# One eighth of w1 by five small loads, and selection tables set up by GpSimd, in a one-token attention and MLP kernel

## The chip, the cores and the metric

The kernel runs on one core of a Trainium2 chip. The metric is the device time of one execution in microseconds (us); the kernel before has a median of 401.98 us over 3 runs (401.95 to 402.12).

## The reference, cut to what matters

One token (`x`, 1024 wide, bf16) goes through an attention with a long cache and, side by side, through an MLP block; the three terms are added.

```python
xn = layernorm(x)
# A: 32 query heads on 4 key/value heads, 65536 cached keys of 128 each
q = xn @ wq                                   # 1024 x 4096
o = softmax(q k^T * 128**-0.5) v              # per head
A = o @ wo                                    # 4096 x 1024
# B: with S = 1
h = gelu(layernorm(xn) @ w1)                  # 1024 x 1024
hs = shift_and_pad(h) @ w2                    # quarters of h shifted by 1, -1, 2, -2 rows: all zero for S = 1
x1 = xn + hs
B = x1 + gelu(layernorm(x1) @ w3) @ w4        # 1024 x 3584, 3584 x 1024
out = x + A + B
```

Nothing is reused between tokens, so every weight and every cached key and value is read from HBM once: 169.87 MB.

## The kernel before, in words

SBUF holds three slots of 64 KB per partition (`SLOTS`, L15; L146). A list of items (L193 to L201) says what passes through them, in this order: `wq`, keys and values of the first half of group 0, `w3`, keys and values of its second half, `wa` (w1 and the first half of w4), then keys and values of the other six half groups, with `wb` (second half of w4, and w2) ahead of the last values, and `wo` last, in five pieces (L17). Each key or value item is 8 MB, 64 KB for each of 128 partitions.

**Loads.** All of them are issued by SyncE (SP) in `load` (L211 to L232, the DMA call itself at L89), in the order of the list, each as soon as the item three places before it has been computed. SP waits until the slot's readers are done (L229) and then issues; so two older loads are normally still queued when a new one is issued. Each `dma_start` adds 16 to a semaphore of its own slot and piece when it has landed. Two small loads of `x` are issued by ScalarE at the start: `x_bf` (L240) into 128 partitions and `xr` (L244) into two partitions, 1 KB each. The result leaves through a store from four partitions (L561).

**Order of engines.** `Flow` records every instruction with what it reads and writes and puts a wait on the engine when the last writer or reader was another engine or a DMA (L41 to L72). Each engine works through its own instructions in the order of the program.

**Items.** For keys, VectorE transposes the slot in blocks (L449), TensorE multiplies with the query (L455), VectorE takes the maximum (L462), ScalarE the exponential (L471), and VectorE transposes the weights (L473); for values, TensorE accumulates (L503). `group_end` (L513) joins the two halves of a group and uses the PSUM tile `pm` (L521 to L526). `compute_wq`, `compute_w3` and `compute_wa` multiply the one row of x, kept spread over partitions in `xpad`, with a weight whose row 8p + c lies in partition p, place c (`rows_product`, L310, matmul at L321): eight places c, and a matmul per place and chunk of 512 columns. In `compute_wa` (L405) this is w1 with 8 x 2 matmuls; then Gelu on ScalarE (L410), a cleared row on GpSimd (L411), a spreading matmul with `gsel` (L419), and the first half of w4 in a loop (`rows_loop`, L326, matmul at L337).

**Set-up.** GpSimd clears tiles and makes two identities (L243 to L260). VectorE makes masks (L265 to L274), then from the bf16 identity the selection tables `psel` (L278, four copies), `hstrip` (L283) and `gsel` (L285). `psel` is first read by the matmul at L368, `hstrip` at L394, `gsel` at L419.

**The end.** `compute_wo` (L541) takes the five pieces of wo as they land; after the last piece come four matmuls (L536), one VectorE copy (L560) and the store (L561).

Of the kernel before, what the change touches and what calls it, by code (L numbers as in the profile page):

```python
# [7 lines left out]
BF16 = mybir.dt.bfloat16  # L8
# [8 lines left out]
WO_PIECES = (10, 10, 8, 3, 1)  # L17
WO_UNROLL = 5
CGS = 2


class Flow:
# [51 lines left out]
    def op(self, eng, reads, writes, emit, times=1):  # L74

        self._wait(eng, reads, writes)
        sem = self.sem(eng)

        def signal(ins):
            ins.then_inc(sem, 1)  # L80

        emit(signal)
        self.counts[eng] += times
        self._note((eng, self.counts[eng]), reads, writes)
# [8 lines left out]
    def one(self, eng, reads, writes, call):  # L93
        self.op(eng, reads, writes, lambda signal: signal(call(self.engines[eng])))
# [3 lines left out]
def kernel(  # L98
# [14 lines left out]
    nc = tc.nc  # L113
    P = 128
    S = A_x.shape[1]
    D = A_x.shape[-1]
# [6 lines left out]
    DC = D // P  # L123
# [18 lines left out]
    def tile_sb(shape, dtype, name):  # L142
        return sb.tile(shape, dtype, name=name)
# [9 lines left out]
    ident_bf = tile_sb([P, P], BF16, "ident_bf")  # L153
# [3 lines left out]
    hstrip = tile_sb([P, 192], BF16, "hstrip")  # L157
    gsel = tile_sb([P, P], BF16, "gsel")
# [10 lines left out]
    xn2b = tile_sb([P, DC], BF16, "xn2b")  # L169
# [3 lines left out]
    gT = tile_sb([P, DC], BF16, "gT")  # L173
    o5 = tile_sb([P, 32], F32, "o5")
    oT = tile_sb([P, OC], BF16, "oT")
    rep = msk[0:1].rearrange("p a b -> p (a b)")

    sc = ps.tile([P, HF, 512], F32, name="sc")
    oacc = ps.tile([P, 512], F32, name="oacc")
    pm = ps.tile([P, 512], F32, name="pm")  # L180
# [4 lines left out]
    w3_v = B_w3.rearrange("(p c) f -> p (c f)", c=DC)  # L185
    w4_v = B_w4.rearrange("(m c) n -> m (c n)", c=FC)
    wo_v = A_wo.rearrange("(m c) n -> m (c n)", c=OC)
    w1_v = B_w1.rearrange("(p c) n -> p (c n)", c=DC)
    w2_v = B_w2.rearrange("(m c) n -> m (c n)", c=DC)
    assert sum(WO_PIECES) == OC  # L190
    wo_start = [sum(WO_PIECES[:i]) for i in range(len(WO_PIECES))]
# [13 lines left out]
    fl = Flow(nc, ctx)  # L205
    one, op = fl.one, fl.op
# [4 lines left out]
    def load(i):  # L211
        item, s = items[i], slot_of[i]
        t, kind = slots[s], items[i][0]
        if kind == "wq":
            loads = [(0, wq_v)]
        elif kind == "w3":
            loads = [(0, w3_v)]
        elif kind == "wa":
            loads = [(0, w1_v), (KEYS // 2, w4_v[:, 0:FH * NOUT])]
        elif kind == "wb":  # L220
            loads = [(0, w4_v[:, FH * NOUT:FC * NOUT]), (KEYS // 2, w2_v)]
        elif kind == "wo":
            loads = [(wo_start[q] * NOUT, wo_v[:, wo_start[q] * NOUT:(wo_start[q] + n) * NOUT])
                     for q, n in enumerate(WO_PIECES)]
        else:
            cache = A_k_cache if kind == "K" else A_v_cache
            _, g, r = item
            loads = [(0, cache[0, g, r * KEYS:(r + 1) * KEYS, :].rearrange("(p k) d -> p (k d)", p=P))]
        fl._wait("Q", [], [("slot", s), ("slot", s, 1)] + [("slot", s, q) for q in range(2, 5)] + [("kt", s, cg) for cg in range(4)])  # L229
        for n, (at, src) in enumerate(loads):  # L230
            key = ("slot", s) if n == 0 else ("slot", s, n)
            fl.dma("Q", f"slot{s}" if n == 0 else f"slot{s}_{n}", [], [key], t[:, at:at + src.shape[-1]], src)  # L232

    qrow = work[:, 0:1024].rearrange("p (b n) -> p b n", b=2)
    psel = work[:, 1024:1536].rearrange("p (b m) -> p b m", b=4)
    ones_f = og[:, 0:P]
    xr = work[:, 1536:2048]

    load(0)
    fl.dma("S", "x", [], ["x_bf"], x_bf[:], A_x[0, 0, :].rearrange("(p c) -> p c", c=DC))  # L240
    load(1)
    load(2)
    one("G", [], ["xr"], lambda e: e.memset(xr[0:33, :], 0.0))  # L243
    fl.dma("S", "x2", [], ["xr"], xr[0:33:32, :], A_x[0, 0, :].rearrange("(j n) -> j n", j=2))  # L244
# [17 lines left out]
    def v(reads, writes, call):  # L262
        one("V", reads, writes, call)
# [10 lines left out]
                                                   in_=sel8[:].unsqueeze(2).to_broadcast([P, 8, 4])))  # L274
    iv = ident_bf[:].rearrange("p (b i r) -> p b r i", b=2, r=2)
    for b in range(2):
        for par in range(2):
            v(["ident_bf"], [("psel", b, par)], lambda e: e.tensor_copy(  # L278
                out=psel[:, 2 * b + par, :].rearrange("p (a i) -> p a i", a=4),
                in_=iv[:, b, par, :].unsqueeze(1).to_broadcast([P, 4, 32])))  # L280
    psel_keys = [("psel", b, par) for b in range(2) for par in range(2)]
    lead = ident_bf[:].rearrange("p (j u) -> p j u", u=32)[:, :, 0]
    v(["ident_bf", "hstrip"], ["hstrip"], lambda e: e.tensor_copy(  # L283
        out=hstrip[:, 64:128].rearrange("p (j m) -> p j m", j=4), in_=lead.unsqueeze(2).to_broadcast([P, 4, 16])))
    v(["ident_bf"], ["gsel"], lambda e: e.tensor_copy(  # L285
        out=gsel[:].rearrange("p (j m) -> p j m", j=2), in_=lead[:, 0:2].unsqueeze(2).to_broadcast([P, 2, 64])))

    def layernorm(src, src_key, n):
# [22 lines left out]
    v([("rs", 0)], ["ln_s1"], lambda e: e.tensor_scalar(out=ln_s1, in0=rs1, scalar1=1.0, scalar2=None, op0=ALU.add))  # L311
    v([("neg", 0), ("rs", 0)], ["ln_s2"], lambda e: e.tensor_tensor(out=ln_s2, in0=neg1, in1=rs1, op=ALU.mult))

    def rows_product(s, keys, wt, width, n_chunks):
        def emit(signal):
            for c in range(DC):
                for j in range(4):
                    for bk in range(2):
                        ch = 4 * bk + j
                        if ch < n_chunks:  # L320
                            ins = nc.tensor.matmul(sc[32 * j:32 * j + 32, bk, 0:width], lhsT=xpad[:, c, :],  # L321
                                                   rhs=wt[:, c, ch * width:(ch + 1) * width],
                                                   start=(c == 0), stop=(c == DC - 1), tile_position=(0, 32 * j),
                                                   skip_group_check=True)
            signal(ins)
        op("T", keys + ["xpad"], ["sc"], emit)  # L326

    def rows_loop(lhsT, wt, n, reads, unroll):

        lv = lhsT.rearrange("p (c u) -> p c u", u=unroll)  # L330
        wv = wt.rearrange("p (c u h n) -> p c u h n", u=unroll, h=2, n=NH)

        def emit(signal):
            with nc.tensor.Fori(0, n // unroll) as c:
                for u in range(unroll):
                    for h in range(2):
                        ins = nc.tensor.matmul(psR[0:1, h, :], lhsT=lv[:, bass.ds(c, 1), u],  # L337
                                               rhs=wv[:, bass.ds(c, 1), u, h, :],
                                               start=False, stop=False, skip_group_check=True)
                signal(ins)  # L340
        op("T", reads, ["psR"], emit, times=n // unroll)
# [62 lines left out]

    def compute_wa(s):  # L405
        slot = slots[s]
        wt = slot[:, 0:DC * D].rearrange("p (c n) -> p c n", n=D)
        rows_product(s, [("slot", s)], wt, 512, 2)
        h1row, grow = work[0:64, 0:512], work[0:64, 512:1024]
        one("S", ["sc"], ["h1row", "work"], lambda e: e.activation(out=h1row, in_=sc[0:64, 0, :], func=ACTF.Gelu_apprx_tanh))  # L410
        one("G", [], ["grow", "work"], lambda e: e.memset(grow, 0.0))  # L411
        cq = D // 4
        for grp, shift in enumerate((1, -1, 2, -2)):
            for t in range(S):
                if 0 <= t - shift < S:
                    r0, c0 = 32 * (grp // 2), cq * (grp % 2)
                    v(["h1row", "grow"], ["grow"], lambda e: e.tensor_copy(
                        out=grow[r0:r0 + 1, c0:c0 + cq], in_=h1row[r0:r0 + 1, c0:c0 + cq]))
        one("T", ["grow", "gsel"], ["pm"], lambda e: e.matmul(pm[:], lhsT=gsel[0:64, :], rhs=grow, start=True, stop=True))  # L419
        gm = work[:, 1024:2048].bitcast(F32).rearrange("p (a c) -> p a c", c=DC)  # L420
        v(["pm", "mask64"], ["gm"], lambda e: e.tensor_tensor(
            out=gm, in0=pm[:].rearrange("p (a c) -> p a c", c=DC),
            in1=mask64[:].unsqueeze(2).to_broadcast([P, 64, DC]), op=ALU.mult))
        v(["gm"], ["gf"], lambda e: e.reduce_sum(out=lnb[:, 7], in_=gm.rearrange("p a c -> p c a"), axis=AX.X))
        v(["gf"], ["gT"], lambda e: e.tensor_copy(out=gT[:], in_=lnb[:, 7]))
        rows_loop(hT[:, 0:FH], slot[:, KEYS // 2:KEYS // 2 + FH * NOUT], FH, ["hT", ("slot", s, 1)], unroll=2)
# [15 lines left out]
    def compute_K(s, g, r):  # L442
        n_cg = 1 if (g, r) == (HKV - 1, NT - 1) else CGS
        kt = slots[s]
# [96 lines left out]
    def compute_wo(s):  # L541
        for q, n in enumerate(WO_PIECES):
# [14 lines left out]
            if q == 1:  # L557
# [4 lines left out]
        fl._wait("G", ["out"], [])  # L562

    compute = {"wq": compute_wq, "w3": compute_w3, "wa": compute_wa, "wb": compute_wb, 
               "K": compute_K, "V": compute_V}
    for i, it in enumerate(items):
# [39 lines left out]
```

## Time and profile before

| what | value |
|---|---|
| median of 3 runs | 401.98 us |
| profiled execution, its own time | 402.23 us |
| span of that execution in the trace | 400.1 us |
| HBM read, mean rate over the span | 169.87 MB, 425 GB/s |
| main DMA queue (q1), share of 16 engines | 98.3% |
| busy: PE, DVE, ACT, POOL | 223.5, 210.5, 30.9, 6.3 us |
| last piece of wo issued to landed | 28.4 us |

How to read it: a profile page gives one execution. Its own time is 2.1 us more than its span (the first to the last instruction), and 0.25 us above the median of the runs. "DMA share" is the mean busy share of the core's 16 DMA engines. The trace holds besides, for every DMA packet, its queue, start, duration and size, and for every transfer the moments at which its engines reported it landed (16 for a load over 128 partitions).

### The profile page before, as it was taken

To read this page: it belongs to the slowest core of one execution; us is meant where nothing else is said; L and a number is where in the kernel's file an instruction comes from. 1 tells how busy PE (TensorE), PEld (TensorE's weight loads), DVE (VectorE), ACT (ScalarE), POOL (GpSimd) and SP (SyncE) were. 2 spreads that over 40 slices of the span, in tenths; PEclk is the share of its full clock that TensorE was granted. 3 is DMA by queue.
4 is the path that set the end of the run, shared out by engine and by line. 5 is a ranking of instruction groups with operands and counts; after the bars stand their busy time and mean duration, and the time that the engine had idled before them with its cause. 6 is when DMAs were issued, how large, how long until landed. Compare 5 with 4: busy or idle time off the path is not lost.

```text
span 400.1 us, 4118 instructions
## 1 busy us (share of the span) xinstructions
PE 223.5 (56%) x1407; PEld 91.3 (23%) x1407; DVE 210.5 (53%) x191; ACT 30.9 (8%) x36; POOL 6.3 (2%) x28
## 2 busy tenths in 40 slices
PE   0263087360195563964395608845925194596985
PEld 0220033130042220421142203312402041232332
DVE  2201792210962448822972499269455963794421
ACT  1000000320001300003001000020020002000200
POOL 3000000000000000000000000000000000000000
PEclk9995579585589598795699567968988599799799
DMA  8999999999989999999999999999999999999995
GB/s 347 465 446 419 420 414 454 391 473 452 426 382 471 451 426 414 426 432 432 465 434 426 419 426 439 426 472 428 426 419 434 439 419 459 398 454 434 397 432 208
DMA packets 4054, 170.02 MB, mean 425 GB/s; under 512 B 582, under 2 KB 588, under 8 KB 844
## 3 DMA queue, kind: packets, MB, share of 16 engines
q1 hardware_dynamic: 3896, 169.87, 98.3%
q8 instruction: 8, 0.13, 0.1%
q10 hardware_dynamic: 148, 0.00, 0.0%
q14 instruction: 2, 0.02, 0.0%
HBM read 169.87 MB, written 0.00 MB: 425 GB/s over the span
## 4 chain that ended last, share of the span: by engine, by line
DMA 53%; PE 28%; DVE 13%; issue 4%; ACT 1%; SPq 1%; POOL 0%; ACTq 0%
DMA slot<-in_A_k_cache_dram 46%; PE sc L455 20%; DVE slot L449 10%; DMA slot<-in_A_wo_dram 7%; PE oacc L503 5%; PE psR L337 2%; DVE sm L462 2%; DVE work L473 1%; ACT work L471 1%; SPq L89 1%; PE sc L321 0%; DVE og L515 0%; ACT L471 0%; DVE sm L464 0%; PE pm L463 0%
## 5 line engine op out<-in xcount | busy, mean ns | idle before, releaser
L455 PE MATMUL sc<-slot,qst 128*128 x512 | 127.8, 407 | 77.4 <-DVE slot L449 76.4
L449 DVE STREAM_TRANSPOSE slot<-slot 128x4096 f32<-128x4096 f32 x32 | 139.4, 4413 | 29.7 <-DMA slot<-in_A_k_cache_dram 29.7
L455 PEld LDWEIGHTS sc<-slot,qst 128*128 128x128 bf16 x512 | 51.8, 101 | 154.2 <-issue 106.8
L503 PE MATMUL oacc<-slot,work 128*32 128x512 bf16 x512 | 45.7, 530 | 37.5 <-DVE work L473 21.9
L462 DVE TENSOR_REDUCE sm<-sc 128x1 f32<-128x2048 f32 x8 | 18.3, 2291 | 58.4 <-PE sc L455 58.4
L503 PEld LDWEIGHTS oacc<-slot,work 128*32 128x32 bf16 x512 | 19.0, 127 | 60.8 <-issue 56.9
L473 DVE STREAM_TRANSPOSE work<-work 128x2048 bf16<-128x2048 bf16 x8 | 18.5, 2312 | 21.2 <-ACT work L471 21.2
L471 ACT ACTIVATE work<-sc,sm 128x2048 bf16<-128x2048 f32 x8 | 15.7, 1967 | 147.1 <-DVE sm L469 147.1
L337 PE MATMUL psR<-slot,hT 128*1 x56 | 16.2, 438 | 0.5 <-issue 0.2
L515 DVE SCALAR_TENSOR_TENSOR og<-oacc,sm,og 128x128 f32<-128x128 f32 x16 | 5.6, 351 | 18.6 <-PE oacc L503 18.2
L321 PE MATMUL sc<-slot,xpad 128*32 128x512 bf16 (+1 forms) x144 | 11.1, 441 | 4.3 <-DMA slot<-in_A_wq_dram 4.3
L471 ACT ACT_TABLE_LOAD x3 | 3.8, 1283 | 117.5 <-DVE sm L469 117.5
L463 PE MATMUL pm<-ident_f,sm 128*1 128x128 f32 x8 | 2.2, 270 | 19.1 <-DVE sm L462 19.1
L294 PE MATMUL pm<-sm,og 128*128 128x1 f32 x4 | 1.2, 363 | 14.9 <-DVE sm L293 14.9
L337 PEld LDWEIGHTS psR<-slot,hT 128*1 x56 | 5.1, 92 | 10.9 <-issue 7.8
L321 PEld LDWEIGHTS sc<-slot,xpad 128*32 128x32 bf16 x144 | 5.4, 113 | 9.0 <-DMA slot<-in_A_wq_dram 4.4
L399 DVE TENSOR_TENSOR work<-pm,mask 128x448 f32<-128x448 f32 x1 | 0.6, 624 | 11.0 <-PE pm L394 11.0
L463 PEld LDWEIGHTS pm<-ident_f,sm 128*1 128x1 f32 x8 | 0.6, 79 | 23.0 <-DVE sm L462 23.0
L352 DVE CAST work<-sc 128x512 bf16<-128x512 f32 x1 | 0.7, 690 | 9.2 <-PE sc L321 9.2
L347 POOL COPY qst<-qsel 32x32 bf16<-32x32 bf16 x12 | 2.5, 206 | 189.0 <-PE sc L455 161.8
L337 PE MATMUL psR<-slot,oT 128*1 x20 | 4.5, 379 | 1.6 <-DVE oT L529 1.6
L509 ACT COPY ob<-oacc 128x512 f32<-128x512 f32 x4 | 2.3, 585 | 33.1 <-PE oacc L503 33.1
(99 smaller groups left out, 71.6 us busy)
## 6 DMA issues: line engine op xcount, KB each, us to landing
slot<-in_B_w_dram SPq DMA_DIRECT2D x1, 7168.0 KB, 50.8
slot<-in_B_w_dram SPq DMA_DIRECT2D x2, 3584.0 KB, 31.9
slot<-in_A_wo_dram SPq DMA_DIRECT2D x2, 2560.0 KB, 19.5
slot<-in_B_w_dram SPq DMA_DIRECT2D x2, 2048.0 KB, 30.1
slot<-in_A_wo_dram SPq DMA_DIRECT2D x1, 2048.0 KB, 26.7
slot<-in_A_wo_dram SPq DMA_DIRECT2D x1, 768.0 KB, 28.1
slot<-in_A_wo_dram SPq DMA_DIRECT2D x1, 256.0 KB, 28.4
slot<-in_A_k_cache_dram SPq DMA_DIRECT2D x8, 36.1
```

Source lines behind the costliest of these rows:

```text
L89: self.engines[eng].dma_start(out=out, in_=in_).then_inc(sem, 16)
L321: ins = nc.tensor.matmul(sc[32 * j:32 * j + 32, bk, 0:width], lhsT=xpad[:, c, :], rhs=wt[:, c, ch * width:(ch + 1) * width], start=(c == 0 ...
L337: ins = nc.tensor.matmul(psR[0:1, h, :], lhsT=lv[:, bass.ds(c, 1), u], rhs=wv[:, bass.ds(c, 1), u, h, :], start=False, stop=False, skip_gr ...
L347: lambda e: e.tensor_copy(out=qst[g % 2][sl, :, 24 + 32 * a:24 + 32 * a + 8], in_=qsel[sl, :, 8 * g:8 * g + 8]))
L449: v([("slot", s)], [("kt", s, cg)], lambda e: e.transpose(out=kf[:, cg, :], in_=kf[:, cg, :]))
L455: ins = nc.tensor.matmul(sc[:, bass.ds(hf, 1), :], lhsT=qst[g % 2][:, bp, 24 - 8 * cg:24 - 8 * cg + P], rhs=kr[:, cg, bass.ds(hf, 1), :, b ...
L462: v(["sc"], ["mx"], lambda e: e.reduce_max(out=mx, in_=sc[:].rearrange("p h n -> p (h n)"), axis=AX.X))
L463: one("T", ["mx", "ident_f"], ["pm"], lambda e: e.transpose(pm[0:1, 0:P], mx, ident_f[:]))
L471: one("S", ["sc", ("nball", r)], WORK + [("lall", r)], lambda e: e.activation(out=pT, in_=sc[:], func=ACTF.Exp, bias=nball[:, r:r + 1], sc ...
L473: v(["work"], ["work"], lambda e: e.transpose(out=pT, in_=pT))
L503: ins = nc.tensor.matmul(oacc[32 * u:32 * (u + 1), :], lhsT=pT[:, hf, 32 * t:32 * (t + 1)], rhs=vt[:, :, hf, t, :], start=(hf == 0 and t < 4),
L515: v(["oacc", ("wm", 1), "og"], ["og"], lambda e: e.scalar_tensor_tensor(out=og[:, 0:P], in0=oacc[:, P * cg:P * (cg + 1)], scalar=wm[:, 1, ...
```

## The change

w1 has eight rows in each partition. The load of 128 partitions now brings seven of them (14 KB for each partition instead of 16 KB). The eighth rows, 128 rows of 2 KB, are brought behind it by five more loads into the same slot, past the place where the eight rows ended: four of five partitions with six rows each (partitions a, a+4, ..., a+16 for a = 0 to 3), and one of four partitions with two rows each. So row p of these lands in another partition than before; the matching elements of the normed x are moved there by eight small matmuls with columns of the identity into `pm` and two VectorE copies into a new tile `xe`. The product with w1 then has 7 x 2 matmuls over 128 partitions and 8 x 2 over 20 or 4 partitions. The five loads share one semaphore (`few`), for which TensorE waits as well. And the six copies that make `psel`, `hstrip` and `gsel` go from VectorE to GpSimd.

```diff
+XP = 20
+XR = 6
+    xe = tile_sb([P, 8], BF16, "xe")
-    w1_v = B_w1.rearrange("(p c) n -> p (c n)", c=DC)
+    w1_v = B_w1.rearrange("(p c) n -> p (c n)", c=DC)[:, 0:(DC - 1) * D]
+    w1_last = B_w1.rearrange("(p c) n -> p c n", c=DC)[:, DC - 1, :]
+    X_AT = DC * D
...
+            if kind == "wa" and n == 0:
+                few = w1_last[0:XP * XR].rearrange("(i a r) n -> a i r n", a=4, r=XR)
+                for a in range(4):
+                    fl.dma("Q", "few", [], [("slot", s, 2)],
+                           t[a:a + XP - 3:4, X_AT:X_AT + XR * D].rearrange("p (r n) -> p r n", n=D), few[a])
+                fl.dma("Q", "few", [], [("slot", s, 2)], t[0:4, X_AT + XR * D:X_AT + (XR + 2) * D].rearrange("p (r n) -> p r n", n=D),
+                       w1_last[XP * XR:P].rearrange("(p r) n -> p r n", r=2))
...
-            v(["ident_bf"], [("psel", b, par)], lambda e: e.tensor_copy(
+            one("G", ["ident_bf"], [("psel", b, par)], lambda e: e.tensor_copy(
...
-    v(["ident_bf", "hstrip"], ["hstrip"], lambda e: e.tensor_copy(
+    one("G", ["ident_bf", "hstrip"], ["hstrip"], lambda e: e.tensor_copy(
...
-    v(["ident_bf"], ["gsel"], lambda e: e.tensor_copy(
+    one("G", ["ident_bf"], ["gsel"], lambda e: e.tensor_copy(
...
-    def rows_product(s, keys, wt, width, n_chunks):
+    def rows_product(s, keys, wt, width, n_chunks, n_c=DC, more=()):
...
-            for c in range(DC):
+            for c in range(n_c):
...
+            for lhsT, c in more:
+                for j in range(n_chunks):
+                    ins = nc.tensor.matmul(sc[32 * j:32 * j + 1, 0, 0:width], lhsT=lhsT,
+                                           rhs=wt[0:lhsT.shape[0], c, j * width:(j + 1) * width],
+                                           start=False, stop=(c == DC + XR + 1), tile_position=(0, 32 * j),
+                                           skip_group_check=True)
...
-        rows_product(s, [("slot", s)], wt, 512, 2)
+        wt = slot[:, 0:X_AT + (XR + 2) * D].rearrange("p (c n) -> p c n", n=D)
+        last = xn2b[:, DC - 1:DC]
+        def emit(signal):
+            for r in range(XR):
+                nc.tensor.matmul(pm[0:XP, r:r + 1], lhsT=ident_bf[:, r:XP * XR:XR], rhs=last, start=(r == 0), stop=False,
+                                 skip_group_check=True)
+            for r in range(2):
+                ins = nc.tensor.matmul(pm[0:4, XR + r:XR + r + 1], lhsT=ident_bf[:, XP * XR + r:P:2], rhs=last, start=False,
+                                       stop=(r == 1), skip_group_check=True)
+            signal(ins)
+        op("T", ["xn2b", "ident_bf"], ["pm"], emit)
+        v(["pm"], ["xe"], lambda e: e.tensor_copy(out=xe[0:XP, 0:XR], in_=pm[0:XP, 0:XR]))
+        v(["pm"], ["xe2"], lambda e: e.tensor_copy(out=xe[0:4, XR:XR + 2], in_=pm[0:4, XR:XR + 2]))
+        rows_product(s, [("slot", s), ("slot", s, 2), "xe", "xe2"], wt, 512, 2, n_c=DC - 1,
+                     more=[(xe[0:XP if r < XR else 4, r:r + 1], DC + r) for r in range(XR + 2)])
```

In the built program SP's queue has, in place of the one load of 128 x 8192 elements, a load of 128 x 7168, four of 5 x 6 x 1024 and one of 4 x 2 x 1024, all ahead of the load of w4.

More of the change, by code (lines that the diff above doesn't have):

```diff
@@ L187 @@
     wo_v = A_wo.rearrange("(m c) n -> m (c n)", c=OC)
-    w1_v = B_w1.rearrange("(p c) n -> p (c n)", c=DC)
+    w1_v = B_w1.rearrange("(p c) n -> p (c n)", c=DC)[:, 0:(DC - 1) * D]
+    w1_last = B_w1.rearrange("(p c) n -> p c n", c=DC)[:, DC - 1, :]
+    XT = P - XP * XR
+    assert XT == 8
+    X_AT = DC * D
     w2_v = B_w2.rearrange("(m c) n -> m (c n)", c=DC)
@@ L228, in load @@
             loads = [(0, cache[0, g, r * KEYS:(r + 1) * KEYS, :].rearrange("(p k) d -> p (k d)", p=P))]
-        fl._wait("Q", [], [("slot", s), ("slot", s, 1)] + [("slot", s, q) for q in range(2, 5)] + [("kt", s, cg) for cg in range(4)])
+        fl._wait("Q", [], [("slot", s), ("slot", s, 1), ("slot", s, 2)] + [("slot", s, q) for q in range(3, 5)] + [("kt", s, cg) for cg in range(4)])
         for n, (at, src) in enumerate(loads):
@@ L406, in compute_wa @@
         slot = slots[s]
-        wt = slot[:, 0:DC * D].rearrange("p (c n) -> p c n", n=D)
-        rows_product(s, [("slot", s)], wt, 512, 2)
+        wt = slot[:, 0:X_AT + (XR + 2) * D].rearrange("p (c n) -> p c n", n=D)
[13 more added lines that the diff above has]
+                     more=[(xe[0:XP if r < XR else 4, r:r + 1], DC + r) for r in range(XR + 2)])
         h1row, grow = work[0:64, 0:512], work[0:64, 512:1024]
```

## The prediction

> **What bounds the kernel now.** I read the page's slices and queues first, then the chain that ended last, then the trace's packet records.
>
> ```profile
> DMA  8999999999989999999999999999999999999995
> ...
> q1 hardware_dynamic: 3896, 169.87, 98.3%
> q8 instruction: 8, 0.13, 0.1%
> ...
> q14 instruction: 2, 0.02, 0.0%
> ...
> DMA 53%; PE 28%; DVE 13%; issue 4%; ACT 1%; SPq 1%; POOL 0%; ACTq 0%
> ```
>
> DMA is busy in all slices but the last, and one queue, SP's loads, holds 98.3% of the time of 16 engines. The 28% of PE in the chain is not a limit: the chain steps from a computed item to the load that it frees, while two older loads are still moving. So the end is set by bytes per DMA engine, and the question is how even the 16 engines are. The windows at the end (us, then PE, PEld, DVE, ACT, POOL, granted clock, DMA share, GB/s) show it:
>
> ```profile
> 394.00:394.40 0.40, 0.32 (x12) 0.29 (x16) 0.00 (x0) 0.00 (x0) 0.00 (x0) 1.00 1.01 410
> ...
> 394.80:395.20 0.40, 0.33 (x12) 0.03 (x4) 0.00 (x0) 0.00 (x0) 0.00 (x0) 1.00 0.48 200
> ...
> 395.60:396.00 0.40, 0.07 (x4) 0.07 (x8) 0.00 (x0) 0.00 (x0) 0.00 (x0) 1.00 0.45 174
> 396.00:396.40 0.40, 0.40 (x12) 0.13 (x12) 0.00 (x0) 0.00 (x0) 0.00 (x0) 1.00 0.07 26
> ```
>
> The share falls to about half at 394.6 and stays there for 1.4 us. The sixteen landings of the last load say the same: seven at 394.66 to 395.18, nine at 396.11 to 396.60.
>
> Why nine are late, the packet records tell. A 64 KB packet starts every 2.418 us on each engine, the next following within some ns, so I can follow end to start and split the records into sixteen streams of 216 data packets each. In eight of these a 16 KB packet of queue q8 (instruction fetch; at 56.2, 87.6, 151.9, 209.7, 272.2, 306.0, 363.2 and 394.6) stands between the data: about 0.93 us, and the data packet behind it takes 2.9 us instead of 2.418. That is 1.4 us, once for each stream. A ninth stream has the two 8 KB packets of q14 (46.3 and 381.0). Seven have none. Their data ends at 394.33 to 394.89, that of the nine at 395.6 to 396.20. No stream idles longer than 0.1 us at a time. I call them the free and the late engines; the gap of some 1.5 us is all that there is to win by balance.
>
> After the last landing nothing moves: four matmuls, one copy, the store, to 400.1.
>
> ```profile
> 396.65 0.28 PE L536 MATMUL sc<-slot,oT 128*1 128x256 bf16 x4 [0.21 <-DMA slot<-in_A_wo_dram]
> 396.98 0.42 DVE L560 CAST ob<-sc 97x256 bf16<-97x256 f32 x1 [4.26 <-PE sc L536]
> 397.43 0.65 SPq L89 DMA_DIRECT2D out_dram<-ob  x1
> ```
>
> **The change, part by part.**
>
> *What each DMA engine carries.* Over 128 partitions an engine has eight. It loses 8 x 2 KB of w1. In the streams, packets of 16384, 28672 and 65536 bytes step by 607, 1059 and 2418 ns, a line of 36.8 ns per 1000 bytes and some 5 ns fixed; 14336 bytes then step by 532 ns, an estimate. All sixteen gain 8 x (607 - 532) = 0.60 us.
>
> Five-partition loads: the trace has none over five partitions. It has one over two (xr), whose two 1 KB packets sit in two different streams, and the store over four, whose four packets overlap in time. So I take one engine per partition: five engines get 4 x 6 = 24 packets of 2 KB, four of these two more. A 2 KB packet steps by 80 ns (last piece of wo). 26 x 80 = 2.08 us, and 5 x 6 ns at the ends of loads, 2.11 us; less 0.60, **+1.51 us on four engines**, +1.34 on the fifth, -0.60 on eleven. Bounds for 2 KB: 75.6 ns (1/32 of 2418) and 86 ns (twice the 43 ns of xr's 1 KB), so +1.36 to +1.67; 80 is the same size and is taken.
>
> The Trainium skill ("DMA: Bandwidth & Descriptors", section on why a DMA increments its semaphore by 16) says that such a load runs on the largest divisor up to 16 of its outer size, and on the lowest-numbered engines. With xr the trace agrees (two streams, the first and second to start).
>
> *Which engines.* The streams that carried xr are the first and second to start on wq, and both are free (394.54 and 394.43). By order of first packets (2.02 to 2.92 us) the free ones are 1st, 2nd, 3rd, 5th, 7th, 9th and 15th; the first five of those end at 394.33 to 394.62. I take these for the five.
>
> *The sum.* Heavy engines: 394.62 + 1.51 = 396.13. Late ones: 396.20 - 0.60 = 395.60. The end of data was 396.20, so the gain is 0.07 us: the load that is shifted is nearly the whole gap, and the heavy engines become last where the late ones were. Bounds: if the seventh free engine (394.89) is among the four, 396.40, +0.2; with 75.6 ns, -0.2.
>
> *SP.* Five more issues at 0.33 to 0.45 us each, ahead of w4:
>
> ```profile
> 83.21 0.33 SPq L89 DMA_DIRECT2D slot<-in_A_v_cache_dram  x1
> 86.26 0.80 SPq L89 DMA_DIRECT2D slot<-in_B_w_dram  x2
> 124.76 0.33 SPq L89 DMA_DIRECT2D slot<-in_A_k_cache_dram  x1
> ```
>
> w4 is issued at about 89 instead of 86.7; keys and values in front of it land until 118, so some 29 us cover it. Behind it on SP nothing waits before 124.76.
>
> *TensorE and VectorE in wa.*
>
> ```profile
> 142.69 1.89 PE L321 MATMUL sc<-slot,xpad 128*32 128x512 bf16 x15
> 142.89 0.15 DVE L523 RECIPROCAL sm<-pm 32x1 f32<-32x1 f32 x1 [0.50 <-PE pm L521]
> 143.08 0.34 DVE L524 SCALAR_TENSOR_TENSOR msk<-pm,sm,mask 32x128 f32<-32x128 f32 x1
> ...
> 153.83 0.33 SPq L89 DMA_DIRECT2D slot<-in_A_k_cache_dram  x1
> ```
>
> The eight moving matmuls write `pm`, so they now wait for L524 (143.42 instead of 142.74: 0.7 us); like L359's eight they take 0.36; two copies behind L527 and L529, some 0.45 past them, 0.6; 14 more matmuls with w1 at 1.89/15 = 0.126 give 1.8. Some 3.5 us. Queued behind: Gelu, the cleared row, the w4 loop, and SP's next issue (153.83, then about 157.3). The values ahead of that load land at 168.6 to 170.6, so 11 us of cover remain; VectorE's transposes of the next keys start at about 151.8 instead of 151.11. Cost nothing; without the cover, 3.5 us. All small loads land some 2 us after w1 (123.3), 17 us before TensorE asks for them.
>
> *Selections on GpSimd.*
>
> ```profile
> 4.20 0.74 DVE L278 COPY work<-ident_bf 128x128 bf16<-128x128 bf16 x4
> ...
> 13.41 0.17 DVE L306 CAST lnb<-x_bf 128x8 f32<-128x8 bf16 x1 [8.24 <-DMA x_bf<-in_A_x_dram]
> ...
> 30.42 0.27 PE L368 MATMUL pm<-qT,work 128*128 128x32 bf16 x4 [0.33 <-DVE qT L363]
> ```
>
> VectorE loses 1.1 us ahead of 8.2 us of waiting for x: nothing gained. GpSimd is done with its clears at 4.44 and next needed at 31.1. Six copies cost between 0.2 us each (L347 on GpSimd, 32 x 32) and 1 us each (twice its 512-element clears, 0.52): done by 10.5 at the latest, 20 us before L368. Nothing.
>
> **The sum:** 402.23 - 0.07 = 402.16 for the profiled execution; against the median, 0.25 lower, **401.9 us**.
>
> **Rivals.**
>
> *One of the five is a late engine (slower).* Nothing but starting order names the third to fifth engine. If a stream that was fetched into is among them, it ends at 395.8 to 396.2 plus 1.34 to 1.51, hence 397.2 to 397.7: 1.0 to 1.5 us later, 402.9 to 403.5. It decides as soon as one such engine is hit. For it: nine of sixteen are late, and the fourth to start is one. Against: the two known ones are free, and the fetches fall into sets by starting order (the first four into the 11th, 12th, 14th and 16th, the next four into the 4th, 6th, 8th and 10th), as if one block of eight took all of them and the loads' first engines were the other block.
>
> *Small loads are dearer.* Each five-partition load of 60 KB could pay a start-up on its engines. In the streams a load's first packet follows the last of the load before within 10 ns, for 256 KB loads too; but none was smaller. At 0.1 to 0.2 us for each of five, +0.4 to +0.9: 402.3 to 402.8.
>
> The skill's page (same title, sections on bandwidth and on the anatomy of one DMA) says, of loads issued from GpSimd, that under 64 KB the descriptors dominate and that each has about 2 us fixed; five in a row would by that make 412 us, an estimate. The back-to-back packets speak against it.
>
> *Balance pays fully.* If the heavy engines stay under the lightened late ones, the most is 0.60 us: 401.4. That needs heavy engines 0.5 us earlier than counted; nothing shows it.
>
> *It doesn't do what it says.* All five partitions on one engine: 120 packets x 80 ns less 0.6 = 9 us on a free engine, 394.5 + 9, 409. xr and the store speak against it. A ninth instruction fetch (TensorE has 22 more of 939 written matmuls) would put 1.4 us on a lightened late engine: 397.0, +0.8.
>
> **Chances.** Forecast (401.6 to 402.2) 0.63; a late engine hit 0.13; dearer loads 0.12; full balance 0.07; the last two 0.05. A measurement can tell about 0.2% (0.8 us) from no change: faster by more 0.03 (even full balance stays under it), within 0.81, slower 0.16. The range runs from full balance, 401.4, to the dear end of the small loads, 402.8; what lies above it is the late engine and the last rivals, 0.18.
>
> **What would show it.** Right: q8 still 8 packets; in the last load's landings four or five engines last, some 1.5 us behind the few remaining free ones, and the nine 0.3 to 0.6 before them; DMA share 1 until about 394; L368 not waiting for GpSimd; SP's issue after wa at about 157. Wrong: landings that end past 397, q8 at 9 packets, 2 KB steps well over 80 ns, or a stretch of DMA under 0.95 around 118 to 130 or 157 to 171.

## The result and the profile after

The changed kernel takes **414.54 us** (median of 6 runs, 414.20 to 415.04) against 402.1 us before (6 runs): ratio 1.0308, 95% interval 1.0297 to 1.0319. The forecast was 401.9 us, with a range of 401.4 to 402.8. The profiled execution took 414.77 us, its span is 413.0 us.

The page after, with the slices, the queues and the chain:

```profile
span 413.0 us, 4173 instructions
...
DMA  9999999999962999999999999999999999999994
...
q1 hardware_dynamic: 4048, 169.87, 95.7%
q8 instruction: 8, 0.13, 0.1%
...
DMA 54%; PE 27%; DVE 13%; issue 3%; ACT 1%; SPq 0%; POOL 0%; ACTq 0%
```

The bytes are the same and q8 still has eight packets. The row of slices has a hole at the 12th and 13th (a slice is 10.3 us): the DMA engines stood nearly still, where before no slice but the last was under 8. The chain that ended last does not show it: its shares are within a point of those before. Windows over the hole (columns as in the prediction):

```profile
118.00:120.00 2.00, 2.00 (x11) 0.87 (x9) 0.00 (x0) 0.00 (x0) 0.00 (x0) 1.00 1.03 423
120.00:122.00 2.00, 2.00 (x10) 0.86 (x9) 0.00 (x0) 0.00 (x0) 0.00 (x0) 1.00 0.51 212
122.00:124.00 2.00, 2.00 (x11) 0.88 (x10) 0.00 (x0) 0.00 (x0) 0.00 (x0) 1.00 0.01 5
124.00:126.00 2.00, 1.24 (x6) 0.37 (x4) 0.72 (x1) 0.00 (x0) 0.50 (x3) 1.00 0.10 31
126.00:128.00 2.00, 0.27 (x1) 0.08 (x1) 1.64 (x2) 0.00 (x0) 0.31 (x2) 0.94 0.09 31
128.00:130.00 2.00, 0.26 (x1) 0.17 (x1) 0.58 (x3) 0.96 (x1) 0.00 (x0) 0.50 0.04 10
130.00:132.00 2.00, 0.00 (x0) 0.00 (x0) 0.00 (x0) 1.99 (x2) 0.00 (x0) 0.50 0.05 20
132.00:134.00 2.00, 0.00 (x0) 0.00 (x0) 1.58 (x1) 0.39 (x2) 0.00 (x0) 0.50 0.89 238
```

The kernel before in two of the same windows:

```profile
122.00:124.00 2.00, 2.00 (x11) 0.86 (x9) 0.00 (x0) 0.00 (x0) 0.00 (x0) 1.00 1.10 475
126.00:128.00 2.00, 0.32 (x2) 0.14 (x2) 1.49 (x3) 0.00 (x0) 0.00 (x0) 1.00 1.00 430
```

One minus the share, times 2 us, summed from 120 to 134, is 10.6 us: so long did an engine stand still in the mean. The last column of the fourth to seventh row says what did move: 10 to 31 GB/s, a small load at a time. The waits of SP's queue (for what, us in total, times, longest), and then SP's issues (start, us), say why:

```profile
SPq L91 <- DMA slot<-in_B_w_dram: 41.9, 4, 36.0
```

```profile
82.38 0.33 SPq L91 DMA_DIRECT2D slot<-in_A_v_cache_dram  x1
85.42 46.65 SPq L91 DMA_DIRECT2D slot<-in_B_w_dram  x7
132.19 0.35 SPq L91 DMA_DIRECT2D slot<-in_A_k_cache_dram  x1
```

Four times SP waited at L91, the issue of a DMA, for a load of B's weights; 36.0 us the longest. The seven issues (w1, five small ones, w4) took from 85.42 to 132.07. One by one, the trace has w1 at 85.42, the small loads at 85.8, 122.79, 125.54, 128.17 and 130.91, and w4 at 131.63. The reason stands in the kernel. All five small loads name the same key, `("slot", s, 2)`, in what they write. `Flow.dma` (L86 of the kernel before) looks up the last writer of each written key, finds the small load just issued, and puts a wait for its landing on SP. That makes four waits. The first small load lies in SP's queue behind w1, which lands at 121.0 to 122.8, and it is the last one queued, so the first of these waits (to 122.8) outlasts all that was queued. Each further wait is a round of issue, transfer and landing, 2.7 us. And w4 and the next keys, which would have filled the queue, stand behind these waits on SP.

The Trainium skill ("DMA: Bandwidth & Descriptors", section on the anatomy of one DMA) says that DMA engines wait on no semaphore and that a wait is done by the issuing sequencer before it dispatches. The trace agrees: the 41.9 us are SP's.

### The profile page after: what moved, and what is told of

The parts are those of the page before. It is cut to its first block, busy times and chain, and to the rows that moved or that the text cites. A ratio compares the mean times of both kernels' runs of the same rounds, so it can differ in the third digit from the quotient of the medians.

```text
span 413.0 us, 4173 instructions
## 1 busy us (share of the span) xinstructions
PE 224.9 (54%) x1429; PEld 91.2 (22%) x1429; DVE 209.9 (51%) x187; ACT 30.9 (7%) x36; POOL 7.7 (2%) x34
## 4 chain that ended last, share of the span: by engine, by line
DMA 54%; PE 27%; DVE 13%; issue 3%; ACT 1%; SPq 0%; POOL 0%; ACTq 0%
DMA slot<-in_A_k_cache_dram 47%; PE sc L489 20%; DVE slot L483 10%; DMA slot<-in_A_wo_dram 7%; PE oacc L537 4%; PE psR L357 2%; DVE sm L496 2%; DVE work L507 1%; ACT work L505 1%; PE sc L341 0%; PE sc L335 0%; SPq L91 0%; DVE og L549 0%; ACT L505 0%; PE sc L570 0%
## 5 line engine op out<-in xcount | busy, mean ns | idle before, releaser
L489 PE MATMUL sc<-slot,qst 128*128 x512 | 130.6, 414 | 86.5 <-DVE slot L483 85.6
L537 PE MATMUL oacc<-slot,work 128*32 128x512 bf16 x512 | 41.3, 494 | 37.8 <-DVE work L507 21.9
L537 PEld LDWEIGHTS oacc<-slot,work 128*32 128x32 bf16 x512 | 17.7, 121 | 58.6 <-issue 52.1
L357 PE MATMUL psR<-slot,hT 128*1 x56 | 14.7, 407 | 0.2
L335 PEld LDWEIGHTS sc<-slot,xpad 128*32 128x32 bf16 x142 | 5.0, 117 | 10.3 <-DMA slot<-in_A_wq_dram 4.4
L570 PE MATMUL sc<-slot,oT 128*1 128x256 bf16 x88 | 4.1, 307 | 2.8 <-DMA slot<-in_A_wo_dram 2.8
```

The costliest lines, as they stand in the source:

```text
L489: ins = nc.tensor.matmul(sc[:, bass.ds(hf, 1), :], lhsT=qst[g % 2][:, bp, 24 - 8 * cg:24 - 8 * cg + P], rhs=kr[:, cg, bass.ds(hf, 1), :, b ...
L537: ins = nc.tensor.matmul(oacc[32 * u:32 * (u + 1), :], lhsT=pT[:, hf, 32 * t:32 * (t + 1)], rhs=vt[:, :, hf, t, :], start=(hf == 0 and t < 4),
L570: ins = nc.tensor.matmul(psB[32 * j:32 * j + 1, 0:NQ], lhsT=lhsT, rhs=w_row[:, NQ * j:NQ * (j + 1)], start=(not started[j]), stop=False, t ...
```

## The experiments

Times are medians, with the ratio to the kernel before, run on the same chip, and its 95% interval.

| run | us | ratio |
|---|---|---|
| small loads without waits | 403.97 | 1.0038 (1.0024 to 1.0052) |
| selections alone | 402.29 | 1.0000 (0.9991 to 1.0009) |
| one wait | 408.95 | 1.0165 (1.0149 to 1.0181) |
| wait alone, no small load | 406.23 | 1.0095 (1.0079 to 1.0110) |
| covered wait | 402.35 | 1.0003 (0.9994 to 1.0012) |
| six engines, without waits | 403.45 | 1.0032 (1.0020 to 1.0043) |
| marks on engines | 402.65 | one run |
| extra load on the first engine | 402.73 | 1.0015 (1.0006 to 1.0024) |
| extra loads on three engines | 402.21 | 1.0001 (0.9992 to 1.0010) |
| extra loads on four engines | 403.69 | 1.0036 (1.0022 to 1.0051) |
| shift to three engines, without waits | 402.72 | 1.0013 (1.0004 to 1.0023) |

### The waits

**Small loads without waits.** From the changed kernel; SP's wait for a free slot and the product with w1 name the five keys.

```diff
-                    fl.dma("Q", "few", [], [("slot", s, 2)],
+                    fl.dma("Q", "few", [], [("few", s, a)],
...
-                fl.dma("Q", "few", [], [("slot", s, 2)], t[0:4, X_AT + XR * D:X_AT + (XR + 2) * D].rearrange("p (r n) -> p r n", n=D),
+                fl.dma("Q", "few", [], [("few", s, 4)], t[0:4, X_AT + XR * D:X_AT + (XR + 2) * D].rearrange("p (r n) -> p r n", n=D),
```

> The changed kernel, with a key of its own for each of the five small loads, so that SP issues them without waiting for one another; bytes, packets, engines and the selections on GpSimd are those of the changed kernel. Theory A (SP's four waits, each for the landing of the small load before, held back the load of w4 and emptied the DMA engines): the whole loss goes, and what is left is the shift of bytes as predicted, 401.6 to 402.4 us, with SP's issues of w1 to w4 within 5 us of each other. Theory B (small loads over five partitions are dear in themselves, waits or not): 405 to 414 us. Theory C (the selections on GpSimd): 414 us.

403.97 us: 10.6 us of the 12.4 us are gone, as much as the hole held. SP's seven issues, and the windows where the hole was:

```profile
86.09 4.83 SPq L91 DMA_DIRECT2D slot<-in_B_w_dram  x7
```

```profile
120.00:122.00 2.00, 2.00 (x11) 0.86 (x9) 0.00 (x0) 0.00 (x0) 0.00 (x0) 1.00 1.00 395
122.00:124.00 2.00, 2.00 (x11) 0.86 (x9) 0.00 (x0) 0.00 (x0) 0.00 (x0) 1.00 1.04 437
```

The issues take 4.83 us and the share stays at 1. But 403.97 is not the 401.6 to 402.4 that theory A gave: 1.5 us above the kernel before stay (by the ratio; 1.7 by the medians, 402.25 us before on that chip), and have another cause (below).

**Selections alone.** The kernel before with six times `one("G", ...)` for `v(...)`, as in the diff of the change.

> The kernel before, with the six copies for the selections moved to GpSimd and nothing else. Theories A and B: within 0.3 us of the kernel before, 401.8 to 402.4 us. Theory C: a good part of the 12.4 us.

402.29, no difference (1.0000). In the changed kernel's timeline GpSimd's copies end at 5.8, 25 us before their first reader (at 31.0):

```profile
4.39 0.99 POOL L292 COPY work<-ident_bf 128x128 bf16<-128x128 bf16 x4
5.33 0.23 POOL L297 COPY hstrip<-ident_bf 128x64 bf16<-128x64 bf16 x1
5.50 0.29 POOL L299 COPY gsel<-ident_bf 128x128 bf16<-128x128 bf16 x1
```

**One wait.** The kernel without waits, with the second small load given the key of the first.

```diff
-                    fl.dma("Q", "few", [], [("few", s, a)],
+                    fl.dma("Q", "few", [], [("few", s, (0, 0, 2, 3)[a])],
```

> As the kernel without waits, but the second small load waits for the landing of the first, as in the changed kernel; the other three wait for nothing. Theory A: SP is free at 122.8, issues the other four by 126, and w4's first packets start at about 126.5 instead of 132.4, so some 6 of the 12.4 us remain: 407 to 409 us. If each wait cost the same, 3.1 us: 405. Theory B: no different from the kernel without waits.

408.95, as theory A gave: the first wait costs 5.0 us over the kernel without, the other three 5.6 together. SP issued the second small load at 122.56 and w4 at 125.57; its first packet started at 126.63, against 132.68 in the changed kernel and 120.72 without waits.

**Wait alone, no small load.** The kernel before, with SP waiting for w1's landing ahead of the load of w4.

```diff
+            if kind == "wa" and n == 1:
+                fl._wait("Q", [("slot", s)], [])
```

> The kernel before, without any small load, but SP waits for the landing of w1 (about 123.3) before it issues the load of w4. Theory A in its general form (any wait of SP for the landing of the load just issued, with nothing else queued, empties the engines): the engines idle from the end of w1 (some at 120.8 to 121.5, the late ones at 122.9) to about 124.2, so +2.5 to +3.3 us: 404.5 to 405.5 us. Theory B: 402.1 us, since no load is small.

406.23, +4.0 us (1.0079 to 1.0110), more than the 2.5 to 3.3 of theory A, and nothing like theory B. SP waited 37.2 us; w4's first packet started at 124.19 instead of 121.15. What the expectation left out: before, 14 of 16 engines had landed w4 between 129.94 and 130.87; now all land at 133.69 to 134.22, so those 14 lose 3.4 to 3.7 us. The first packets after the stand took longer: 1.2 to 2.2 us for 28 KB, instead of 1.06 before (1.3 to 2.1 in the changed kernel).

**Covered wait.** The same place, but waiting for the keys two items earlier.

```diff
+            if kind == "wa" and n == 1:
+                fl._wait("Q", [("slot", slot_of[i - 2])], [])
```

> The kernel before, with a wait of SP ahead of the load of w4 for the landing of the keys two items earlier (at 99), while those values and w1 are still queued behind them up to 122. Theory A: SP stands some 12 us, the DMA engines go on, nothing is lost: 401.9 to 402.5 us. If a wait of SP between loads costs in itself, as much as the one of the kernel that waits for w1 (+4.0 us): 404 to 406 us.

402.35: nothing. SP's issues and waits:

```profile
86.04 13.24 SPq L89 DMA_DIRECT2D slot<-in_B_w_dram  x2
```

```profile
SPq L89 <- DMA slot<-in_A_k_cache_dram: 12.6, 1, 12.6
```

SP stood 12.6 us for a landing, while some 10 MB, the values and w1, were still queued behind that load. So it is not the wait that costs, but the queue that runs dry behind it.

### The 1.5 us that stay

The sixteen landings of the last piece of wo in the kernel without waits are at 394.31 to 394.65 (three), 395.69 to 396.81 (twelve), and one at 398.42. Windows at its end:

```profile
396.40:396.80 0.40, 0.40 (x16) 0.28 (x8) 0.00 (x0) 0.00 (x0) 0.00 (x0) 0.50 0.09 36
396.80:397.20 0.40, 0.40 (x16) 0.28 (x8) 0.00 (x0) 0.00 (x0) 0.00 (x0) 0.50 0.07 31
397.20:397.60 0.40, 0.40 (x16) 0.14 (x4) 0.00 (x0) 0.00 (x0) 0.00 (x0) 0.50 0.04 15
```

A share of 0.04 to 0.07 is one engine of 16. Its data ends at 398.06; the four other loaded engines end at 396.14 to 396.51 (396.13 was forecast). On each of the four engines with 26 small packets these took 2.02 us from the first start to the last, 81 ns each. So the small loads are not dear. But on one of those four they begin at 121.98, on the other loaded engines at 120.90 to 121.27: one engine was late already. In the streams of packets the engine that ends last has the 8 KB packet of q14 at 381.52; for the one at 71.44 the streams are not clear. The changed kernel shows the late engine too: its first small load lands on four engines at 121.62 to 121.83 and on the fifth at 122.77. Six runs test that one of the five engines is a late one.

**Six engines.** The kernel without waits with `XP = 24`, `XR = 5`.

> The kernel without waits, with the small loads over six partitions with five rows each (four of them) and four partitions with two rows. Theory D (the 1.7 us that the kernel without waits is above the one before come from one of the five engines, the one that also carries the two 8 KB packets of q14; small loads are no dearer than 80 ns for 2 KB): that engine, if among the first four, has 22 small packets instead of 26, so its data ends 0.32 us earlier: 403.5 to 403.8 us. Theory E (each small load costs extra on its engines): five loads remain, so nothing changes, 404.0 us. If the sixth engine is one with a 16 KB fetch, it ends at 396.2 + 1.03, under that of theory D, and does not show in the time.

403.45, 0.5 us under five engines (0.3 forecast); the last landing comes 0.4 us earlier, at 398.03. It goes the way of theory D, but the two intervals overlap: not a proof by itself.

**Marks on engines.** The kernel before with loads into unread room, two rows of w1 each.

```diff
+                for a, wide in enumerate((1024, 896, 768, 640)):
+                    fl.dma("Q", "few", [], [("few", s, a)],
+                           t[0:a + 2, x_at:x_at + 2 * wide].rearrange("p (r n) -> p r n", n=wide), rows[0:a + 2, 0:8:4, 0:wide])
+                    x_at += 2 * wide
```

> The kernel before, with four extra small loads behind w1 into room that nothing reads: over 2, 3, 4 and 5 partitions, two rows each, with packets of 2048, 1792, 1536 and 1280 bytes. The sizes mark the engines in the trace. If a load over n partitions always takes the first n engines, one pair of streams carries all four sizes, one more three, one more two, one more one. Theory D: one of these five streams carries q14's two 8 KB packets. Time: at most 0.6 us more on an engine, 402.0 to 402.7 us.

Two streams carry all four sizes. The stream with q14's packet at 46.4 carries 1536 and 1280 bytes and neither 2048 nor 1792: it is in the loads over four and five partitions and not in those over two and three, hence the fourth engine. A few marks were put down to wrong streams, where packets of two engines end within some ns of each other, so this is not yet a proof; the runs with extra loads on three and on four engines are.

**Extra load on the first engine.** The kernel before with three loads of one partition and 17 rows.

```diff
+                for a in range(3):
+                    fl.dma("Q", "few", [], [("few", s, a)],
+                           t[a:a + 1, DC * D:DC * D + 17 * 480].rearrange("p (r n) -> p r n", n=480), B_w1[17 * a:17 * a + 17, 0:480])
```

> The kernel before, with three extra loads behind w1 of one partition and 17 rows of 960 bytes each, into room that nothing reads; 17 has no divisor but itself, so each should lie on one engine, the first: 51 packets at some 40 ns, 2.0 us. If the first engine is the one with q14's packets (data ending at 395.98): 398.0 in place of 396.2, +1.8 us, 404.0. If it is a free one (394.3 to 394.9): 396.3 to 396.9, +0.1 to +0.7 us.

402.73: the first engine is a free one. 45 of the 51 packets fall into one stream, whose data ends at 396.60. The Trainium skill's rule quoted in the prediction (the largest divisor up to 16) makes one engine of 17 rows, and the trace agrees. In this separation into streams it is the last one to start on wq, at 2.72.

**Extra loads on three engines, and on four.** The kernel before with four loads of three (four) partitions and four rows into unread room.

```diff
+                for a in range(4):
+                    fl.dma("Q", "few", [], [("few", s, a)],
+                           t[a:a + 9:4, DC * D:(DC + 4) * D].rearrange("p (r n) -> p r n", n=D), rows[3 * a:3 * a + 3, 0:8:2, :])
```

> The kernel before, with four extra loads behind w1 over three partitions, four rows of 2 KB each, into room that nothing reads: three engines carry 16 small packets more, 1.3 us. Theory D (the fourth engine is the one with q14's packets, the first three are free): the three end at 395.6 to 396.2, under the late engines: 402.1 to 402.5 us. Theory E (each small load costs extra, whatever its engines): as much above the kernel before as with four partitions.

> As the kernel with three partitions, but over four, so that the fourth engine too carries 16 small packets more. Theory D: the fourth engine ends at 395.98 + 1.31 = 397.3 instead of 396.2 for the last: +1.1 us, 403.2 to 403.5 us, and one landing stands alone at the end. Theory E: the same as with three.

402.21 and 403.69: nothing with three, +1.4 us with four (theory D gave +1.1). Windows of the two at the same times, three engines first:

```profile
396.40:396.80 0.40, 0.28 (x8) 0.09 (x4) 0.00 (x0) 0.00 (x0) 0.00 (x0) 1.00 0.00 0
396.80:397.20 0.40, 0.09 (x4) 0.00 (x0) 0.26 (x1) 0.00 (x0) 0.00 (x0) 1.00 0.00 0
```

```profile
396.40:396.80 0.40, 0.40 (x20) 0.18 (x8) 0.00 (x0) 0.00 (x0) 0.00 (x0) 1.00 0.07 31
396.80:397.20 0.40, 0.09 (x4) 0.00 (x0) 0.00 (x0) 0.00 (x0) 0.00 (x0) 1.00 0.04 15
```

With three, all is still at 396.4; with four, one engine goes on, landing at 398.22, 1.5 us behind the next. In the streams of that run the engine that ends last (397.87) carries 16 small packets and both 8 KB packets of q14 (46.45 and 382.08). That it came later than theory D said is in part 0.4 us by which its packets of w4 and of the next keys took longer. Four small loads each time, so theory E falls.

**Shift to three engines, without waits.** `XP = 12`, `XR = 4`, and the other 80 rows by one load over 80 partitions.

```diff
+                fl.dma("Q", "few", [], [("few", s, 4)], t[0:XT, X_AT + XR * D:X_AT + (XR + 1) * D], w1_last[XP * XR:P])
```

> The changed kernel without waits, with 48 of the 128 eighth rows by four loads of three partitions (four rows each) and the other 80 by one load over 80 partitions. Three engines carry 16 + 5 packets of 2 KB for the 0.6 us that they lose, +1.1 us; the other thirteen 5 packets, -0.2 us. Theory D: the three end at 395.7 to 396.0, the late ones at 396.0: 0.2 us under the kernel before, hardly to be told from it, 401.9 to 402.3 us; and 1.5 to 1.9 us under the kernel without waits over five partitions. Theory E: as that kernel, 403.5 to 404.3 us, since it has as many small loads.

402.72, 0.4 us above the kernel before, where 0.2 under it was expected. The last landings lie in one group, 396.81 to 397.35, with none alone; but all sixteen engines are some 1 us later than expected. From 121 to 124, while the load over 80 partitions and w4 ran side by side, most packets of 28 KB took 1.2 to 1.4 us instead of 1.06, and those of 2 KB up to 0.13 instead of 0.084; together 7 us too much, 0.45 for each engine. Ahead of them w1's 14 KB packets took up to 0.77 us instead of 0.535, 5 us too much in all, 0.3 for each engine. Why they slow each other I did not test.

## Why the prediction was wrong, point by point

- **What bounds the kernel: right.** DMA is the limit, and the end is where the slowest engine ends. The late engines and the eight fetches show in each run whose packets I followed.
- **SP: the step that failed.** It said "Five more issues at 0.33 to 0.45 us each" and "some 29 us cover it". It counted five issues and no wait, though the front states that `Flow` waits for the last writer of a key, and the diff gives all five the same key. The four waits are 10.6 of the 12.4 us: without them the kernel takes 403.97; with one, 408.95. What came is the prediction's own sign of being wrong, DMA under 0.95 around 118 to 130. No rival had a wait of SP in it; the dearest figure that it weighed (412 us, for five loads in a row at a fixed cost each) came near the size, but as a cost of each small load, and without the waits the same loads follow one another at 81 ns per packet. The issue itself was mis-sized too: 0.68 to 0.95 us for a small load.
- **What each DMA engine carries: right for the small loads, in part for w1.** 81 ns per 2 KB where 80 was taken; free engines that were loaded ended at 396.14 to 396.51 where 396.13 was forecast. The 0.60 us that all engines were to gain came only in part: w1's 14 KB packets, 535 ns each where nothing slowed them (532 was estimated), were 4.7 us too long in all in the kernel without waits, 0.3 for each engine, but only 0.04 us in all with one wait. The cause is open.
- **Which engines: wrong, and it was the first rival.** "One of the five is a late engine" had 0.13 and +1.0 to +1.5 us; without waits it came out at +1.5, so that even without the waits the time lay above the forecast's range. The fourth engine carries q14's two packets. The order of starting, by which I chose the free engines, names none: in the run with the load on the first engine, that stream started last. The range stopped at 402.8, under this rival.
- **TensorE and VectorE in wa: right.** In the changed kernel:

```profile
142.69 0.34 PE L432 MATMUL pm<-xn2b,ident_bf 128*20 128x1 bf16 x6 [0.62 <-DVE msk L558]
...
143.62 1.69 PE L335 MATMUL sc<-slot,xpad 128*32 128x512 bf16 x14 [0.55 <-DVE xe L440]
145.24 1.89 PE L341 MATMUL sc<-slot,xe 20*1 20x512 bf16 x16
```

  The wait for L558 (the old L524), the eight small matmuls, the copies and sixteen more products are there, and SP's issue after wa came at 156.55 (about 157 was forecast), covered. That it came so close is in part luck: in the kernel without waits it came at 161.20, since the matmuls took twice the time (3.17 us for fourteen) at a granted clock of 0.50 from 144 to 152, where the changed kernel had 1.00 until 148. There, too, it was covered: the values ahead landed at 171.5.
- **Selections on GpSimd: right.** 1.0000.

No version here beats the kernel before. Balance could win 0.6 us at most by the forecast's own bound. The fourth engine is a late one, and small loads began at the first engine in the runs that mark it, so they spare the fourth only by staying on three.

## What to carry to other kernels

Where a recorder makes waits from names, a name used twice is a wait: read the issue order with its waits, not the diff, before counting issues as cheap. A wait of the loading queue costs nothing while transfers behind the one waited for still fill the engines (12.6 us of waiting, no loss), and the whole refill when it is the last one queued (5.0 us for the first, then some 2 us each). To balance engines, first mark them: give loads over different numbers of partitions different packet sizes, and see which stream carries what.

## What the runs showed of the hardware

- From a landing that SP waits for to the first packet of the next load took 1.5 us (122.77 to 124.30), and a whole round with 60 KB 2.7 us, though a load's six packets on each engine need only 0.48.
- A 60 KB load over five partitions took SP 0.71 to 0.95 us to issue, one of 16 KB over four partitions 0.68, against 0.33 for most loads over 128.
- A stand, in which all engines are still for a while, also evens them out: in the changed kernel fifteen of w4's sixteen landings fall between 142.22 and 142.58, where before they were spread from 129.94 to 131.76. Behind the stand come six 16 KB fetches and one 8 KB packet of q14, and just seven of the last load's landings are late (408.51 to 409.37, the other nine 407.43 to 408.00). So delays of single engines ahead of the stand cost nothing at the end.
- Each 16 KB instruction fetch held one engine for 1.4 us (0.9 itself, 0.5 on the next data packet), on eight different engines, in the kernel before and in the two with extra loads on three and on four engines. The Trainium skill ("Runtime: NRT & Kernel Launch", section on instruction fetch) says that crossing a block is mostly hidden. For the instructions that may be so, no run here shows it; for the data, in this kernel where the DMA engines are the limit, the trace says otherwise: the engines that were fetched into end some 1.5 us after the free ones.
